# A planned attention, Fourier and channel-mixing kernel: weight signs by VectorE on 16-bit halves, the first masks added by TensorE, a new order

## The chip, the cores and the metric

One core of a Trainium2 chip. The metric is the device time of the program in microseconds (us), the median of the runs. Engines are named as the profile names them: PE is TensorE (PEld its weight loads), DVE is VectorE, ACT is ScalarE, POOL is GpSimd, SP is SyncE, which issues nearly all DMAs.

## The reference

```
scores = q @ k.T / 8                       # 8 batches, 8 heads, 576 tokens, 64 wide
scores = where(mask, scores, -1e9)         # heads 0-3: the last 32 tokens; heads 4-7: every 32nd token, both causal
x      = softmax(scores) @ v               # heads side by side: 8 x 576 x 512
u      = x + real(fft(fft(x, axis=tokens), axis=channels))
un     = (u - mean(u)) / sqrt(var(u) + 1e-6)
out    = u + relu(un @ w1) @ w2            # w1 512 x 2048, w2 2048 x 512, both float64
```

## The kernel before

Heads are taken in pairs: pairs 0 and 1 have the local mask, pairs 2 and 3 the strided one. Of eight batches the first three do attention in float32 (`scores32`, `att_first` for batch 0, `att_pair32` for batches 1 and 2), the others with split 16-bit operands. A pair is a chain: load q, k and v; scores on PE (L556); `weigh` on DVE scales the scores in PSUM and adds the mask (L783), takes the maximum of each window (L790) and subtracts it (L792, on DVE or POOL); exp on ACT; turn on PE; copy on ACT; values on PE; normalise on DVE (L807 to L820); store to the scratch tensor xd in DRAM. Pair 1 of batch 0 is called s_1, o_1, xo_1 below.

When all four pairs of a batch are in xd, the batch is read back as `xa`, and in reversed token order as `xb` by four gathers that POOL issues (L867). `fft_batch` forms E = xa + xb and O = xa - xb (L877), folds them, and PE multiplies by the two transform tables (A, L1020 and L1023 for batch 0; then B). The sums give u; `norm` normalises 128 rows, splits them in two 16-bit parts and turns them by DMA (L1141) into uT. A chunk is 256 rows: 8 `up` steps on PE (L1347, tile ph) and 8 `down` steps (L1387, tile acc). There are 18 chunks; from chunk 15 on, the `Folded` form with other products is used.

The weights arrive as float64 words. `weights(wi, i, m)` turns m pieces of 128 x 512 into float32 bits: ACT scales the high words by a power of two (c1, L1180); a shift of the low words (cl, L1184 on ACT or L1186 on DVE); the sign (sg, L1191 on ACT or a copy on DVE), written as 16 bits into the upper half of each low word; and DVE joins the words (c2, L1197). A pair of pieces (m = 2) has 1024 elements to a partition, a single one 512. PE sums squares of them (gram, L1224), and from these scales ACT and DVE split each weight into two 16-bit parts (L1263, L1266 for w1; L1299, L1302 for w2). All of w1 has to be split before all `up` steps of chunk 0 can run, all of w2 before its `down` steps. While a gram bank is open and the planner sees PE idle, `rest` (L1232) puts in matmuls that add zero.

What sets the order: `Order.run`, at build time, takes steps from threads, each step with an engine, a duration from the source, buffers to get and put, and events; it picks the step that can start first, ties within a window settled by each thread's bias. A step with `alt` can go to a second engine if its duration plus a bias is better. Durations and biases stand in the table `P` and in the `op(...)` calls. Every engine then runs its list in that order, so a step waits for all steps listed ahead of it on its engine. While a step of POOL lasts, the planner keeps most DVE steps back.

```
yield op("V", 1.2 if local else 0.97, get="sm", put="big qk", note=f"weigh {nm}")
o = op("A", 1.15 if m == 2 else 0.69, note=f"sg{z} {wi} {i}", alt=dict(V=(0.62 * m, P["Lsg"])))
o = op("G", 3.45, get="f6", sets=f"O{b}", note=f"O {b}", alt=dict(V=(1.78, P["LO"])))
```

Of the kernel before, what the change touches and what calls it, by code (L numbers as in the profile page):

```python
# [288 lines left out]
def body(ctx: ExitStack, tc: tile.TileContext, a, out):  # L289
# [288 lines left out]
    def att_pair32(b, hp):  # L578
# [34 lines left out]
        yield op("V", 1.05 if local else 0.77, note=f"max {nm}")
        next(g_)
        o = op("V", 1.07 if local else 0.8, note=f"sub {nm}", alt=dict(G=(1.9 if local else 1.38, P["Lsub"])))
        yield o
        g_.send(o)
# [44 lines left out]
    def att_first(sp, pw):  # L662
# [50 lines left out]
        def scores(hp, acc):  # L713
            local = hp < 2
            yield op("T", 0.97 if hp < 2 else 0.84, get="acc" if acc else "big", need=f"q{hp}", sets=f"sc{hp}", note=f"scores {hp}")
# [1133 lines left out]
```

## Time and profile before

| | |
|---|---|
| time, median of 3 runs | 954.75 us (951.97 to 955.89) |
| profiled execution | 950.99 us, span of its instructions 949.1 us |
| PE busy | 913.1 us, 96% of the span |
| DVE, ACT, POOL busy | 694.6 us, 524.6 us, 293.9 us |
| mean granted TensorE clock | 0.981 of full speed |
| moved by DMA | 108.40 MB |

The profiled execution is 1.9 us longer than its span, and 3.76 us shorter than the median of the runs. A busy PE includes the matmuls that add zero. The span falls in a stretch up to the first `up` step of chunk 0, in which weights are converted and batch 0 is brought through attention and transform, and a long stretch in which PE works through the chunks with the other batches' attention in between.

### The profile page before, as it was taken

The numbers are of one execution on the slowest core, as the hardware profiler recorded it, in microseconds if no ns is written. First come the engines' busy times: TensorE is split into PE (matmuls) and PEld (weight loads), VectorE is DVE, ScalarE is ACT, GpSimd is POOL, SyncE is SP. The second block draws the span as 40 slices with busy tenths as digits, with TensorE's granted clock in tenths as the row PEclk, the third lists the DMA queues.
The fourth block names the chain that finished last, engine by engine and source line by source line (L and its number), as shares of the span: only waits on it lengthen the run. The fifth ranks groups of instructions, "written<-read, shape, count | busy, mean of one in ns | idle before, by whom it ended". The sixth has DMA issues, their size and how long they took to land.

```text
span 949.1 us, 25301 instructions
## 1 busy us (share of the span) xinstructions
PE 913.1 (96%) x10583; PEld 673.1 (71%) x10585; DVE 694.6 (73%) x1333; ACT 524.6 (55%) x995; POOL 293.9 (31%) x314
## 2 busy tenths in 40 slices
PE   7688989999999999999999999999999999999997
PEld 6566776666776667666776676667766767699986
DVE  5576777768786786749676866595869889978655
ACT  3878976356573655645646565556433444455542
POOL 0110224124322342334224422452144226525120
PEclk9978899999999999999999999999999999999999
DMA  9878366514344634374336263632250102011100
GB/s 302 269 279 255 126 170 219 179 40 148 95 117 116 156 84 123 98 177 94 97 88 185 73 145 87 186 88 95 55 131 1 45 8 56 17 52 25 41 23 23
DMA packets 140370, 108.40 MB, mean 114 GB/s; under 512 B 108256, under 2 KB 118752, under 8 KB 140256
## 3 DMA queue, kind: packets, MB, share of 16 engines
q1 hardware_dynamic: 137696, 98.40, 37.7%
q0 software_dynamic: 2560, 8.39, 2.6%
q8 instruction: 83, 1.36, 0.6%
q14 instruction: 31, 0.25, 0.1%
HBM read 64.26 MB, written 18.89 MB: 88 GB/s over the span
## 4 chain that ended last, share of the span: by engine, by line
PE 86%; ACT 5%; DVE 4%; issue 2%; DMA 2%; POOL 1%; SPq 0%; DVEq 0%; ACTq 0%; POOLq 0%
PE acc L1387 32%; PE ph L1347 32%; PE acc L1674 5%; PE f L1531 3%; PE B L999 2%; PE A L976 2%; PE s L471 1%; PE o L502 1%; DMA q<-in_qk 1%; PE f_0x L1531 1%; PE f_2x L1531 1%; ACT W L1191 1%; ACT sa L1191 1%; PE o L509 1%; PE s L556 1%
## 5 line engine op out<-in xcount | busy, mean ns | idle before, releaser
L1347 PE MATMUL ph<-uT,W 128*128 128x256 f16 x2880 | 328.7, 273 | 0.7 <-DMA uT<-hb 0.7
L1347 PEld LDWEIGHTS <-W 128*128 128x128 f16 x2880 | 278.9, 98 | 42.7 <-DMA uT<-hb 0.8
L1387 PE MATMUL acc<-W,hb 128*128 128x512 f16 x1344 | 302.4, 379 | 0.0
L1366 POOL TENSOR_TENSOR hb<-hf,hb 128x512 f16<-128x512 f32 x112 | 144.5, 1290 | 330.3 <-ACT hb L1364 233.9
L1387 PEld LDWEIGHTS <-hb 128*128 128x128 f16 x1344 | 128.6, 98 | 142.8
L1363 ACT ACTIVATE hf<-ph 128x512 f32<-128x512 f32 x120 | 71.3, 594 | 143.6 <-PE ph L1347 99.5
L1364 ACT ACTIVATE hb<-ph 128x512 f16<-128x512 f32 x112 | 66.3, 592 | 0.0
L1674 PEld LDWEIGHTS <-tail 128*128 128x128 f16 x504 | 48.3, 98 | 6.5 <-issue 1.3
L1441 DVE TENSOR_TENSOR fold<-fold,W 128x512 f32<-128x512 f32 x64 | 51.9, 834 | 0.2
L433 ACT ACTIVATE kt<-qk,sc 128x576 f16<-128x576 f32 (+1 forms) x40 | 29.4, 788 | 13.5 <-DVE sc L389 12.4
L1531 PEld LDWEIGHTS <-tail 128*128 128x128 f16 x576 | 34.6, 98 | 1.7 <-issue 0.7
L1674 PE MATMUL acc<-fold,tail 128*128 128x256 f16 x288 | 35.5, 273 | 0.0
L448 DVE SCALAR_TENSOR_TENSOR kt<-qk,sc,kt 128x576 f16<-128x576 f32 (+1 forms) x40 | 33.2, 869 | 3.2 <-ACT kt L433 3.1
L1100 ACT ACTIVATE pq<-B,fcm 128x128 f32<-128x128 f32 (+7 forms) x105 | 27.2, 382 | 15.1 <-PE B L999 14.2
L1644 DVE TENSOR_TENSOR tail<-hb,tail 128x512 f16<-128x512 f32 (+1 forms) x46 | 31.8, 720 | 3.3 <-ACT tail L1641 3.1
L1232 PE MATMUL gram<-oneb,zero 128*128 128x128 bf16 x386 | 31.9, 251 | 1.2 <-issue 1.1
L989 DVE SCALAR_TENSOR_TENSOR AT<-A,AT 128x290 f16<-128x290 f32 (+3 forms) x35 | 15.2, 481 | 23.5 <-ACT AT L984 20.8
L1618 POOL TENSOR_TENSOR hb<-hb 128x256 f32<-128x256 f32 x20 | 15.8, 796 | 52.7 <-ACT hb L1604 17.2
L1232 PEld LDWEIGHTS <-zero 128*128 128x128 bf16 x386 | 29.5, 116 | 3.3 <-issue 2.5
L1121 POOL TENSOR_TENSOR rstd<-mv,negh 128x1 f32<-128x1 f32 x30 | 20.1, 676 | 34.7 <-DVE mv L1118 30.1
L792 DVE TENSOR_TENSOR sm<-sm,mx 128x594 f32<-128x594 f32 (+1 forms) x32 | 30.2, 942 | 0.4
L1139 DVE TENSOR_TENSOR unp<-un,unp 128x512 f16<-128x512 f32 x28 | 23.1, 825 | 10.0 <-ACT unp L1136 9.9
(306 smaller groups left out, 1516.9 us busy)
## 6 DMA issues: line engine op xcount, KB each, us to landing
qk<-in_qk SPq DMA_DIRECT2D x28, 592.0 KB
out<-ub SPq DMA_DIRECT2D x32, 256.0 KB
sa<-in_w SPq DMA_DIRECT2D x14, 512.0 KB
vn<-in_vl SPq DMA_DIRECT2D x10, 432.0 KB
W<-in_w SPq DMA_DIRECT2D x8, 512.0 KB
xd<-xo SPq DMA_DIRECT2D x16, 256.0 KB
xa<-xd SPq DMA_DIRECT2D x8, 512.0 KB
vn<-in_vs SPq DMA_DIRECT2D x10, 384.0 KB
```

What stands on the lines that cost most here:

```text
L448: V.scalar_tensor_tensor(out=lo, in0=src, scalar=f, in1=hi, op0=ALU.mult, op1=ALU.subtract)
L792: on(o).tensor_tensor(out=sm, in0=sm, in1=mx[:, 0:nb].rearrange("p (g o) -> p g o", o=1).to_broadcast([128, nb, w]), op=ALU.subtract)
L1232: T.matmul(idle[-1][:, 0:128], zerb, oneb, start=False, stop=False)
L1347: T.matmul(ph[:, i, :], W1[:, 4 * (f0 // 512) + d, x, f0 % 512 : f0 % 512 + 128], self.uhl[y][:, d, :], start=(n == 0), stop=(n == 11))
L1363: A.activation(hf, ph, AF.Relu, scale=HS)
L1364: A.activation(hh, ph, AF.Relu, scale=HS)
L1366: G.tensor_tensor(out=hl, in0=hf, in1=hh, op=ALU.subtract)
L1387: T.matmul(self.acc[s], (hh, hl)[x][:, i, 128 * s : 128 * s + 128], W2[:, f, 1 - y, :], start=(f == 0 and n == 0), stop=(f == 15 and n == 2))
L1441: on(e).tensor_tensor(out=w, in0=w if x is None else x, in1=y, op=ALU.add if f else ALU.subtract)
L1531: T.matmul(dst[:, 128 * f : 128 * f + 128], w(x, i)[:, 128 * f : 128 * f + 128], u(y, i), start=opens and f == 0 and n == 0, stop=closes a ...
L1644: on(o).tensor_tensor(out=lo, in0=src, in1=hi, op=ALU.subtract)
L1674: T.matmul(dst, hop[:, x, j, 128 * i : 128 * i + 128], w(y, i), start=bank not in opened, stop=q == 3 and z in (6, 5, 3, 4) and i == 1 and ...
```

## The change

1. `weights`: the sign is no longer a float copy on DVE but, on 16-bit halves, an AND of the highest half of each word with 0x8000, written to the same place. On ACT it stays as it was. The planner's durations for sg become 2.5 (pair) and 1.35 (single) on ACT, 0.7 and 0.46 on DVE.
2. `scores32`: ahead of the scores of a pair PE writes the mask into the PSUM bank by bf16 matmuls of the identity with the mask's upper halves (3 for a local pair, 2 for a strided one), and the scores are added to it. A new function `peak` takes the maximum out of PSUM and subtracts it while leaving PSUM; the factor 0.125 moves into ACT's exp. `weigh` is left to batches 3 to 7. q and k are given back after the scores and not after `weigh`; the PSUM tile is held until the subtraction. The steps of batch 0 now need the identity and the masks to be loaded ahead of the scores.
3. `P` has new numbers throughout: no pairs in w2 (`M1=()`), other staging buffers for w2's pieces (`S1`), the bias LO of O on DVE from -8.618 to 23.142, and others. With it the order of all engines is new.

```
-    WV=0.068, WA=0.22, WG=1.14, WT=0.212, SL=0.0, SLD=1.819, np=3, AL=3.136, SG=2.918, Lcl=0.163, Lsg=2.308, Lfs=-0.071,
-    Lwl=6.215, Lul=-7.046, LO=-8.618, LE=4.916, Lc2=-2.015, LSD=-15.747, Lsub=4.379, Lsub0=20.296, Lrt=11.607, Lu=4.507,
+    WV=0.068, WA=0.04, WG=0.925, WT=0.185, SL=0.0, SLD=0.818, np=3, AL=3.136, SG=2.918, Lcl=-0.177, Lsg=0.763,
+    Lfs=-1.314, Lwl=-2.525, Lul=-9.275, LO=23.142, LE=5.158, Lc2=-1.062, LSD=-13.902, Lsub=20.832, Lsub0=28.983,
...
+        eye = half16(ident)
+        if local:
+            m = half16(mloc.rearrange("p g w -> p (g w)"))
+            masks = [(0, m), (512, m[:, w:]), (512 + 4 * w, m[:, w : 2 * w])]
+        else:
+            m = half16(mstr)[:, 0:GR].rearrange("p (o w) -> p o w", o=1).to_broadcast([128, NG2, w])
+            masks = [(0, m), (512, m)]
+        for o, m in masks:
+            T.matmul(ps[:, o : o + (m.shape[1] if local else per * w)], eye, m, start=o % 512 == 0, stop=False, skip_group_check=True)
...
-                    T.matmul(ps[rows(local, g, h), off[g] : off[g] + w], qk[hs, st : st + 64], qk[hs, S + st : S + st + w], start=True, stop=True)
+                    T.matmul(ps[rows(local, g, h), off[g] : off[g] + w], qk[hs, st : st + 64], qk[hs, S + st : S + st + w], start=False, stop=True, skip_group_check=True)
...
-        yield op("V", 1.2 if local else 0.97, get="sm", put="big qk", note=f"weigh {nm}")
+        yield op("V", 1.1 if local else 0.8, note=f"peak {nm}")
+        g_ = peak(nm, ps, n, wk, lambda: apool.tile([128, NQB * WIN], F32, tag="sm", name=f"sm{nm}", bufs=1))
+        next(g_)
+        yield op("V", 1.15 if local else 0.9, get="sm", put="big", note=f"less {nm}")
...
+    def peak(nm, ps, nb, w, sm):
+        per = (nb + 1) // 2
+        mx = small.tile([128, 2 * NG2], F32, tag="mx", name=f"mx{nm}")
+        pv = ps.rearrange("p (x c) -> p x c", x=2)[:, :, 0 : per * w].rearrange("p x (g w) -> p x g w", w=w)
+        V.tensor_reduce(out=mx[:, 0 : 2 * per].rearrange("p (x g) -> p x g", x=2), in_=pv, axis=AX.X, op=ALU.max)
+        yield sm
+        sm = (sm() if callable(sm) else sm)[:, 0 : nb * w].rearrange("p (g w) -> p g w", w=w)
+        for x, g0, g1 in ((0, 0, per), (1, per, nb)):
+            top = mx[:, g0:g1].rearrange("p (g o) -> p g o", o=1).to_broadcast([128, g1 - g0, w])
+            V.tensor_tensor(out=sm[:, g0:g1], in0=pv[:, x, 0 : g1 - g0], in1=top, op=ALU.subtract)
+        yield sm
...
-        o = op("A", 1.15 if m == 2 else 0.69, note=f"sg{z} {wi} {i}", alt=dict(V=(0.62 * m, P["Lsg"])))
+        o = op("A", 2.5 if m == 2 else 1.35, note=f"sg{z} {wi} {i}", alt=dict(V=(0.7 if m == 2 else 0.46, P["Lsg"])))
...
-            V.tensor_copy(sg, wh.bitcast(F32))
+            ws = stg.bitcast(U16).rearrange("p (n t) -> p n t", t=4)
+            V.tensor_scalar(ws[:, :, 1], ws[:, :, 3], 0x8000, None, op0=ALU.bitwise_and)
```

ACT, from the conversion of the first weights on: W_89 is the staging tile of w1, q_111 and q_113 the next two, L1191 (L1208 in the new numbering) the sign. Before:

```order
L1180 ACTIVATE W_89<-W_89 128x1024
L745 COPY pt_1_123<-pT_1_453 96x1024
L1191 ACTIVATE W_89<-W_89 128x1024
L745 COPY pt_1_123<-pU_1_495 96x128
L1191 ACTIVATE W_89<-W_89 128x1024
L1180 ACTIVATE W_89<-W_89 128x1024
L1184 ACTIVATE W_89<-W_89 128x1024
L1263 ACTIVATE W_89<-W_90,scl 128x2x512 x2
L1191 ACTIVATE W_89<-W_89 128x1024
L1180 ACTIVATE W_89<-W_89 128x1024
L1184 ACTIVATE W_89<-W_89 128x1024
L1191 ACTIVATE W_89<-W_89 128x1024
```

and now:

```order
L750 COPY pt_1_123<-pT_1_416 96x1024
L1198 ACTIVATE W_89<-W_89 128x1024
L750 COPY pt_1_123<-pU_1_463 96x128
L1208 ACTIVATE W_89<-W_89 128x1024
L1198 ACTIVATE W_89<-W_89 128x1024 x2
L1202 ACTIVATE W_89<-W_89 128x1024
L1198 ACTIVATE q_111<-q_111 128x1024
L1202 ACTIVATE q_111<-q_111 128x1024
L1281 ACTIVATE W_89<-W_90,scl 128x2x512 x2
L1198 ACTIVATE q_113<-q_113 128x1024
L1281 ACTIVATE W_89<-W_90,scl 128x2x512 x4
```

Of the signs ACT keeps one pair here. In the whole program ACT had all 23 of them (9 pairs, 14 single) and now has 1 pair and 6 single; DVE has 5 pairs and 14 single.

SP's DMA queue, behind the loads of batch 0: xd_95 is the scratch tensor of batch 0, xo_3, xo_2, xo_0 and xo_1 the finished pairs. Before:

```order
L1168 DMA W_89<-in_w 128x512 x5
L829 DMA xd_95<-xo_3_133 18x11x64 x2
L829 DMA xd_95<-xo_3_133 18x10x64
L829 DMA xd_95<-xo_3_133 18x11x64 x2
L829 DMA xd_95<-xo_3_133 18x10x64
L829 DMA xd_95<-xo_2_132 18x11x64 x2
L829 DMA xd_95<-xo_2_132 18x10x64
L829 DMA xd_95<-xo_2_132 18x11x64 x2
L829 DMA xd_95<-xo_2_132 18x10x64
L1168 DMA W_89<-in_w 128x512
L815 DMA xd_95<-xo_0_130 128x4x128
L817 DMA xd_95<-xo_0_130 64x64 x2
```

and now:

```order
L1186 DMA W_89<-in_w 128x512 x8
L1186 DMA q_111<-in_w 128x512 x2
L847 DMA xd_95<-xo_3_133 18x11x64 x2
L847 DMA xd_95<-xo_3_133 18x10x64
L847 DMA xd_95<-xo_3_133 18x11x64 x2
L847 DMA xd_95<-xo_3_133 18x10x64
L1186 DMA q_113<-in_w 128x512 x2
L847 DMA xd_95<-xo_2_132 18x11x64 x2
L847 DMA xd_95<-xo_2_132 18x10x64
L847 DMA xd_95<-xo_2_132 18x11x64 x2
L847 DMA xd_95<-xo_2_132 18x10x64
L833 DMA xd_95<-xo_0_130 128x4x128
```

All 12 weight loads now stand ahead of the stores of pairs 2, 0 and 1; ten of them stand ahead of the first store, where five did.

DVE at the transform of batch 0 (E, O, tmp and FD are its tiles, L1197 the joining of weight words, L1266 the second half of a split weight). Before:

```order
L1197 SCALAR_TENSOR_TENSOR W_90<-q_111 128x1024
L1266 SCALAR_TENSOR_TENSOR W_89<-W_90,scl,W_89 128x2x512
L877 TENSOR_TENSOR E_752<-xa_591,xb_593 128x1536
L877 TENSOR_TENSOR O_755<-xa_591,xb_593 128x1536
L877 TENSOR_TENSOR tmp_757<-E_752 128x3x255
L1266 SCALAR_TENSOR_TENSOR W_89<-W_90,scl,W_89 128x2x512
L877 TENSOR_TENSOR tmp_757<-tmp_757 128x3x128
L1197 SCALAR_TENSOR_TENSOR W_90<-q_113 128x1024
L877 TENSOR_TENSOR FD_758<-tmp_757 128x3x64 x2
L877 TENSOR_TENSOR E_752<-O_755 128x3x255
L877 TENSOR_TENSOR FD_758<-E_752 128x3x127 x2
L877 TENSOR_TENSOR FD_758<-tmp_757 128x3x128
```

and now:

```order
L1284 SCALAR_TENSOR_TENSOR W_89<-W_90,scl,W_89 128x2x512 x3
L895 TENSOR_TENSOR E_758<-xa_676,xb_678 128x1536
L895 TENSOR_TENSOR tmp_762<-E_758 128x3x255
L895 TENSOR_TENSOR tmp_762<-tmp_762 128x3x128
L895 TENSOR_TENSOR FD_763<-tmp_762 128x3x64 x2
L895 TENSOR_TENSOR E_758<-O_760 128x3x255
L895 TENSOR_TENSOR FD_763<-E_758 128x3x127 x2
L895 TENSOR_TENSOR FD_763<-tmp_762 128x3x128
L1204 TENSOR_SCALAR sa_12_794<-sa_12_794 128x512
L1211 TENSOR_SCALAR sa_12_794<-sa_12_794 128x512
L1215 SCALAR_TENSOR_TENSOR W_90<-sa_12_794 128x512
```

O has left DVE: in all eight batches it stands on POOL, next behind the gathers. No weight step stands between E and the last FD, where one L1266 and one L1197 stood.

On PE the counts are: 30 mask matmuls more, 378 matmuls of L1232 where 386 were, everything else the same in number. Ahead of the first `up` step the scores of pairs 3 and 2 of batch 1 stand as before; those of pair 0 have moved behind it.

## Rows read from the trace of the kernel before

**Rows 1.** The page, part 5 (costliest groups): the matmuls that add zero
```profile
L1232 PE MATMUL gram<-oneb,zero 128*128 128x128 bf16 x386 | 31.9, 251 | 1.2 <-issue 1.1
```

**Rows 2.** Busy time by stretch; columns: stretch, length, engines, PEclk, DMA share, GB/s
```profile
0.00:98.94 98.94, 75.91 (x1031) 61.87 (x1033) 65.25 (x128) 70.04 (x79) 10.50 (x16) 0.84 0.85 277
98.94:180.00 81.06, 76.14 (x906) 56.13 (x905) 59.94 (x114) 55.64 (x80) 22.58 (x20) 0.99 0.53 160
180.00:820.00 640.00, 640.00 (x7095) 445.47 (x7094) 479.87 (x918) 338.01 (x691) 224.60 (x240) 1.00 0.39 100
820.00:949.10 129.10, 121.09 (x1556) 109.61 (x1553) 89.51 (x177) 60.92 (x148) 36.20 (x39) 0.99 0.11 32
```

**Rows 3.** Line L1191, the sign on ACT: ns min/median/max; who waited, us and times
```profile
L1191 ACT ACTIVATE sa<-sa x14: 1329/1348/1409, 65.8 to 114.9; 128x512 f16<-128x512 f32 x14
...
L1191 ACT ACTIVATE W<-W x4: 2472/2490/2501, 26.1 to 41.6; 128x1024 f16<-128x1024 f32 x4
...
  DVE W L1197: 19.9, 17
```

**Rows 4.** DVE groups by line and form, first 180 us: busy us, mean ns
```profile
L792 DVE TENSOR_TENSOR sm<-sm,mx 128x864 f32<-128x864 f32 x6 | 7.3, 1215 | 0.1
L790 DVE TENSOR_REDUCE mx<-sm 128x9 f32<-128x864 f32 x6 | 6.3, 1051 | 0.1
...
L1197 DVE SCALAR_TENSOR_TENSOR W<-W 128x1024 int32<-128x1024 int32 x4 | 4.9, 1226 | 6.5 <-ACT W L1191 6.5
...
L783 DVE SCALAR_TENSOR_TENSOR sm<-s,mloc 128x480 f32<-128x480 f32 x6 | 3.9, 654 | 2.9 <-PE s L556 2.8
...
L1186 DVE TENSOR_SCALAR sa<-sa 128x512 int32<-128x512 int32 x8 | 3.5, 460 | 0.0
L783 DVE SCALAR_TENSOR_TENSOR sm<-s,mloc 128x384 f32<-128x384 f32 x6 | 3.3, 549 | 0.0
...
L1186 DVE TENSOR_SCALAR W<-W 128x1024 int32<-128x1024 int32 x2 | 1.4, 700 | 1.8 <-DMA W<-in_w 1.8
```

**Rows 5.** Timeline of SP's DMA queue and of POOL: start, length, what
```profile
10.08 7.53 SPq L1168 DMA_DIRECT2D W<-in_w  x5
19.00 8.64 SPq L829 DMA_DIRECT2D xd<-xo  x12
...
33.91 1.18 SPq L817 DMA_DIRECT2D xd<-xo  x2
...
39.11 1.14 POOL L867 DMA_INDIRECT xa<-xd,ridx  x1 [36.32 <-DMA q<-in_w]
```

**Rows 6.** From E of batch 0 to the first `up` step: timelines, one stretch
```profile
50.91 1.75 DVE L877 TENSOR_TENSOR E<-xa,xb 128x1536 f32<-128x1536 f32 x1
...
62.46 0.70 PE L1020 MATMUL A<-f32a,FD 33*65 33x290 f32 x2
...
62.40:74.10 11.70, 11.65 (x34) 6.27 (x32) 6.35 (x11) 10.81 (x14) 1.15 (x2) 0.55 0.65 221
...
89.45 0.55 DVE L1129 TENSOR_SCALAR un<-ub,mv,rstd 128x512 f32<-128x512 f32 x1
...
92.34 0.60 ACT L1136 CAST hb<-un 128x512 f16<-128x512 f32 x1
...
98.94 3.82 PE L1347 MATMUL ph<-uT,W 128*128 128x256 f16 x24
```

**Rows 7.** POOL's and DVE's elementwise steps at the same time: line L1366, and timelines
```profile
L1366 POOL TENSOR_TENSOR hb<-hf,hb x112: 1144/1160/3062, 143.5 to 820.2; 128x512 f16<-128x512 f32 x112
...
159.62 1.17 POOL L1366 TENSOR_TENSOR hb<-hf,hb 128x512 f16<-128x512 f32 x1
...
159.69 2.03 DVE L792 TENSOR_TENSOR sm<-sm,mx 128x864 f32<-128x864 f32 x1
```

**Rows 8.** Chain that ended last: twelve matmuls of 512 columns; scores of a local pair
```profile
130.74 1.07 PE s L556 x36
...
164.25 2.59 PE acc L1387 x12
```

More of the change, by code (lines that the diff above doesn't have):

```diff
@@ L15 @@
 U32 = mybir.dt.uint32
+U16 = mybir.dt.uint16
 AF = mybir.ActivationFunctionType
@@ L159 @@
 AL, SG = P["AL"], P["SG"]
-PORT = ("st", "weigh", "max", "out", "AL", "y1", "y2", "norm", "vlo", "fin", "SD", "u0", "u1", "u2", "rstd", "pad", "ones", "zero", "xb", "c5", "scales")
+PORT = ("st", "peak", "less", "weigh", "max", "out", "AL", "y1", "y2", "norm", "vlo", "fin", "SD", "u0", "u1", "u2", "rstd", "pad", "ones", "zero", "xb", "c5", "scales")
 class Op:
@@ L605, in att_pair32 @@
         spawn(values())
-        yield op("T", 0.97 if local else 0.84, get="big", at=end, note=f"scores {nm}", slack=SL)
+        yield op("T", 1.4 if local else 1.16, get="big", put="qk", at=end, note=f"scores {nm}", slack=SL)
         ps = psbig(f"s{nm}")
         wk, off = scores32(ps, qk, local, n)
-        yield op("V", 1.2 if local else 0.97, get="sm", put="big qk", note=f"weigh {nm}")
-        sm = apool.tile([128, NQB * WIN], F32, tag="sm", name=f"sm{nm}", bufs=1)
-        g_ = weigh(nm, ps, local, n, wk, off, 0.125, sm)
+        yield op("V", 1.1 if local else 0.8, note=f"peak {nm}")
+        g_ = peak(nm, ps, n, wk, lambda: apool.tile([128, NQB * WIN], F32, tag="sm", name=f"sm{nm}", bufs=1))
+        next(g_)
+        yield op("V", 1.15 if local else 0.9, get="sm", put="big", note=f"less {nm}")
         sm = next(g_)
[L613 to L617, printed above, removed]
         yield op("A", 0.92 if local else 0.7, get="" if local else "pbt", put="" if local else "sm", note=f"exp {nm}")
         if local:
-            A.activation(sm, sm, AF.Exp)
+            A.activation(sm, sm, AF.Exp, scale=0.125)
             pb, nt = sm, NQB
         else:
-            A.activation(pbd[:, 0:NG, 0:GR], sm, AF.Exp)
+            A.activation(pbd[:, 0:NG, 0:GR], sm, AF.Exp, scale=0.125)
             pb, nt = pbd.rearrange("p (g e) c -> p g (e c)", e=2), NG2
@@ L714, in scores @@
             local = hp < 2
-            yield op("T", 0.97 if hp < 2 else 0.84, get="acc" if acc else "big", need=f"q{hp}", sets=f"sc{hp}", note=f"scores {hp}")
+            yield op("T", 1.4 if hp < 2 else 1.16, get="acc" if acc else "big", need=f"q{hp} id " + ("mloc" if local else "mstr"), sets=f"sc{hp}", note=f"scores {hp}")
             ps = wide(acc, f"s0_{hp}")
@@ L718, in scores @@
             w, off = scores32(ps, q0s[hp], local, nb)
-            yield op("V", 1.2 if local else 0.97, put="acc" if acc else "big", need="mloc" if local else "mstr", note=f"weigh {hp}")
-            g = weigh(f"0_{hp}", ps, local, nb, w, off, 0.125, sms[hp])
+            yield op("V", 1.1 if local else 0.8, note=f"peak {hp}")
+            g = peak(f"0_{hp}", ps, nb, w, sms[hp])
+            next(g)
+            yield op("V", 1.15 if local else 0.9, put="acc" if acc else "big", note=f"less {hp}")
             sm = next(g)
-            yield op("V", 1.05 if local else 0.77, note=f"max {hp}")
-            next(g)
-            o = op("V", 1.07 if local else 0.79, note=f"sub {hp}", alt=dict(G=(1.95 if local else 1.4, P["Lsub0"])))
-            yield o
-            g.send(o)
             yield op("A", 0.93 if local else 0.72, sets=f"e{hp}", note=f"exp {hp}")
             if local:
-                A.activation(sm, sm, AF.Exp)
+                A.activation(sm, sm, AF.Exp, scale=0.125)
                 pbs[hp] = sm
             else:
-                A.activation(pbs[hp][:, 0:NG, 0:GR], sm, AF.Exp)
+                A.activation(pbs[hp][:, 0:NG, 0:GR], sm, AF.Exp, scale=0.125)
                 pbs[hp] = pbs[hp].rearrange("p (g e) c -> p g (e c)", e=2)
@@ L788, in weigh @@
         yield sm
-        mx = small.tile([128, NG], F32, tag="mx", name=f"mx{nm}")
+        mx = small.tile([128, 2 * NG2], F32, tag="mx", name=f"mx{nm}")
         V.tensor_reduce(out=mx[:, 0:nb], in_=sm, axis=AX.X, op=ALU.max)
```

22 lines of the change are left out of this document (11 added, 11 removed).

## The prediction

> **What bounds the kernel now.** I read the busy times by stretch first [rows 2]. From 180 to 820 us PE is busy in every one of the 640 us, so there the time is the sum of PE's work, and a faster DVE or ACT gives nothing. PE stands idle only ahead of that: 98.94 - 75.91 = 23.0 us up to the first `up` step of chunk 0, 81.06 - 76.14 = 4.9 us from there to 180, and 129.1 - 121.1 = 8.0 us after 820, most of it behind the last matmul. To the 23.0 come 31.9 us of matmuls that add zero [rows 1], nearly all in the first stretch, and the clock granted there, 0.84 of full speed. So whatever this change can win is won by letting the first `up` step start ahead of its 98.94 us; what it can lose anywhere is PE work added, or a PE wait made, after that.
>
> In the first stretch no engine is full: ACT is busy for 70.0 of 98.9 us, DVE for 65.3, and DMA for 0.85 of the time [rows 2]. The order of a chain across them decides, and ACT's longest steps are in it: a sign takes ACT 2.49 us for a pair and 1.35 for a single piece, and DVE's joining of the words waited 19.9 us in 17 waits for it [rows 3].
>
> **The change, part by part.**
>
> *Signs.* ACT loses 9 pairs and 14 singles and keeps 1 and 6: 8 x 2.49 + 8 x 1.35 = 30.7 us less. On DVE 5 pairs and 14 singles are new. No row shows that operation (an AND, two bytes written in every eight). The nearest is L1186, DVE's shift of one operand with a constant on the same tile and step: 0.70 and 0.46 us; the upper end for DVE is L1197, which takes one element at a time, 1.23 us, and far beyond it ACT's own 2.49 [rows 3, 4]. I take L1186: 5 x 0.70 + 14 x 0.46 = 9.9 us more for DVE.
>
> *Masks.* Twelve matmuls of 512 columns take 2.59 us, 0.216 each [rows 8]. A local pair adds 480 + 384 + 96 = 960 columns, 0.41 us; a strided one 2 x 324 = 648, 0.27 us. Ahead of the first `up` step these stand in PE's idle time. After it are the scores of pairs 0 and 1 of batch 1 and of four pairs of batch 2: 4 x 0.41 + 2 x 0.27 = **2.2 us** of PE work in the full stretch. That the scores now wait for masks to load costs nothing in batch 0: pair 0's mask is issued between q of pairs 0 and 1, and PE has pair 1's q to wait for anyway.
>
> *DVE in attention.* A local pair costs 0.654 + 0.549 + 1.051 + 1.215 = 3.5 us [rows 4]. Now it is a maximum out of PSUM over 960 elements, which no row shows: between 1.05 us (864 elements, SBUF) and 1.2 us (that, scaled by 960/864), I take 1.16; and two subtractions out of PSUM at the L783 prices, 1.20. That is 1.1 us less for each of six local pairs, and an estimated 0.7 for each of six strided ones (594 elements). All in all 11 us, which pays for DVE's signs. Off the path, both count nothing by themselves.
>
> *Path to E.* In the new queue ten weight loads are ahead of the first store of batch 0 and twelve ahead of the last. Loads went out at 7.53/5 = 1.51 us, stores at 8.64/12 = 0.72, the last small ones at 0.59 [rows 5]. From 10.08: ten loads to 25.1, six stores to 29.5, two loads to 32.5, six stores to 36.8, six small ones to 40.3. Before, the last store was out at 33.91 + 1.18 = 35.1 and the gathers began 4.0 us later, at 39.11 [rows 5]. If loads past the fifth find room sooner, the last store is out at about 35 again. So the gathers come 0 to 5.2 us later, less up to 2 because no load is left just ahead of the last stores. I take E 1 us later than 50.91 (range -2 to +5). DVE's own queue ahead of E now holds five signs, one L1197 and three L1266 more, 8.6 us, less 3.6 for four shorter pairs; I count the 5 us as worked off while DVE would have waited for ACT's signs, and the range covers it otherwise.
>
> *E to A.* From E to A before: 62.46 - 50.91 = 11.55 us [rows 6]. L1197 and L1266 no longer stand in it (1.23 + about 1.28), and O's 1.75 us leave DVE: 7.3. But O now runs on POOL next to E. The trace shows what that does: a subtraction on DVE that began 0.07 us after a step of POOL took 2.03 us, the other five of its form (7.3 - 2.03) / 5 = 1.05; it waited out POOL's step [rows 4, 7]. O on POOL lasts, from 1.16 us for 512 elements [rows 7], up to 3 x 1.16 = 3.5 us, and not under DVE's 1.75; I take 3.2, and half of it, 1.5 us, as DVE's wait. E to A: 8.8 us. The Trainium skill, "SBUF — State Buffer", section "Who interferes with whom", says the same and speaks against this move: a DVE instruction with two SBUF inputs and a GpSimd instruction that reads SBUF hold the same port for the whole instruction, and the one that issues second "fully blocks". By it all of O's 3.2 us could fall on DVE and A come 1.7 us later than I have it; without it A would come 1.5 us sooner. The row agrees, by one case of 0.98 us. A starts at 50.91 + 1 + 8.8 = 60.7, **1.8 us sooner**.
>
> *A.* From 62.4 to 74.1 the granted clock is 0.55 of full speed, that is 1.2 GHz for nearly all of it, with PE busy throughout [rows 6]; before it PE had stood idle in short gaps between added zeros. At 2.4 GHz the 11.65 us would be 0.55 x 11.65 = 6.4. The new list has 146 matmuls of zero directly ahead of A where 8 behind 27 stood, so the clock may be up; or a gap still follows. 0 to 5.2 us, I take half, **2.6 us**.
>
> *A to the first `up` step.* 98.94 - 74.1 = 24.8 us. In it, `un` of the second half was done at 89.45 + 0.55 = 90.0, and ACT came to its cast at 92.34, from signs and scalings queued ahead [rows 6]: 2.3 us. Sums of u and the scaling of AT stood behind the same steps. Between 1 us (DVE's new work takes half back) and 7, I take **4 us**.
>
> *After the first `up` step.* ACT was busy 55.6 of 81 us [rows 2], most of it in the first third; with four signs fewer here I give PE 1.5 of its 4.9 us idle. Against that stand the masks, 2.2 us, and the scores of pair 0 of batch 1, moved behind the first `up` step: 1.07 us [rows 8].
>
> Sum: -1.8 - 2.6 - 4.0 = -8.4, so the first `up` step at 90.5; -8.4 - 1.5 + 2.2 + 1.0 = -6.7. The profiled execution of 950.99 would take 944.3. It lies 3.76 below the median of 954.75, so for the median of the runs: **948 us**.
>
> What is late next: the split of w2 ahead of `down`. It has the conversion of 12 pieces behind the first `up` step in both lists, and PE has 12 `up` steps and batch 1's attention to do until then, where it had 10.
>
> **The rivals.**
>
> *A, the front is held by transfers.* The stores go out 5.2 us later, A keeps its slow clock. Then E to A as above gives A 2.4 us later than before, -4 behind it, the first `up` step at 97.3: -1.6 - 1.5 + 3.2 = 0.1, the median at 955. For it: DMA is at 0.85 in the first stretch. Against it: the same weights have to come either way, and the loads sent early are the ones the split needs. Chance 0.22.
>
> *B, all of it comes.* Gathers 2 us sooner (A 4.8 sooner), full clock 5.2, 7 us behind A: -17, with 3 us less idle and 3.2 more work -16.8 at most, 938; of the usual size 942. Chance 0.12.
>
> *C, slower: the sign costs DVE what it costs ACT,* because what makes ACT's 2.49 us out of the 1.2 of a plain pass is the narrow write, which stays. Five pairs ahead of E cost 5 x 1.79 = 9.0 us, two singles on the way to the `up` step 1.8: -8.4 + 10.8 = +2.4. Nine more behind it are 8 us on a DVE that is busy for 59.9 of 81 us [rows 2], of which I let 3 reach PE: 2.4 + 3 - 1.5 + 3.2 = +7, 962. It decides from about 1.9 us a pair on. Against it: the slowest of DVE's own forms at this size is at 1.23 us [rows 4]. Chance 0.07.
>
> *D, a bank held longer.* The scores' PSUM tile was free after `weigh`, 1.2 us, and is now held through maximum and subtraction, 2.36. There are two such banks, and PE's next step of attention needs one. If PE waits the 1.16 us for each of the eight pairs of batches 1 and 2, 9.3 us go: +2.6, 957. Against it: `up` and `down` steps lie between, and PE had no wait of this kind in the full stretch. Chance 0.10, a part of it with further stalls and over 959.5.
>
> **How the numbers follow.** My forecast has 0.49, with its own range 944 to 952 from the ends of E, clock and O. A measurement of this kernel can tell about 0.5%, 4.8 us, from no change: faster is under 950.0, slower over 959.5. Faster: 0.45 of the forecast and all of B, 0.57. Same: 0.04 of the forecast, A's 0.22 and 0.06 of D, 0.32. Slower: C and 0.04 of D, 0.11. For the range I reach to B's usual size and beyond A and D's plain case: 940 to 957.
>
> **What would show it.** Right: the first `up` step at 88 to 93 us, A at 60 to 62 with a granted clock over 0.7, the sign on DVE at 0.7 and 0.46 us, ACT busy some 31 us less, DVE some 14 us less (O's eight go to POOL), no PE idle from 180 to 820. Wrong: the first `up` step at 96 or later (A); a sign over 1.9 us (C); waits of PE for DVE's subtraction (D); or PE idle inside the full stretch, which none of my terms has.

## The result and the profile after

The changed kernel takes 964.44 us (median of 4 runs, 963.98 to 965.10); the kernel before took 953.36 us beside it (4 runs, 951.75 to 955.89). The ratio is 1.0114, with a 95% interval of 1.0087 to 1.0142: the change makes it **slower by 1.1%**, 11 us. Forecast were 948 us, within 940 to 957. The profiled execution of 964.66 us has a span of 962.6 us, 13.5 us more than the span before, and a mean granted clock of 0.975.

The page of after, part 1, busy time by engine:

```profile
PE 923.9 (96%) x10605; PEld 675.2 (70%) x10607; DVE 720.2 (75%) x1333; ACT 494.9 (51%) x983; POOL 342.2 (36%) x326
```

ACT is busy 29.7 us less, as forecast (31). DVE is busy 25.6 us more, where 14 less were forecast. PE is busy 10.8 us more and idle 38.7 us instead of 36.0.

Where the time lies is read from the busy time by stretch of after (columns as in [rows 2]):

```profile
0.00:95.31 95.31, 75.34 (x997) 59.90 (x1000) 69.56 (x130) 45.95 (x61) 16.27 (x17) 0.82 0.77 258
95.31:180.00 84.69, 78.96 (x945) 57.30 (x943) 63.05 (x110) 50.42 (x82) 25.54 (x19) 0.98 0.57 180
180.00:260.00 80.00, 80.00 (x892) 55.59 (x890) 61.98 (x126) 42.35 (x93) 35.28 (x39) 1.00 0.42 117
260.00:280.00 20.00, 17.31 (x190) 12.65 (x190) 12.58 (x35) 13.10 (x35) 4.97 (x8) 0.91 0.36 88
280.00:420.00 140.00, 140.00 (x1688) 96.81 (x1687) 101.68 (x195) 76.04 (x148) 48.54 (x46) 1.00 0.45 111
420.00:440.00 20.00, 17.27 (x157) 9.92 (x155) 6.52 (x10) 6.17 (x12) 8.52 (x9) 0.91 0.67 191
440.00:820.00 380.00, 380.00 (x4095) 263.58 (x4094) 298.42 (x538) 192.99 (x395) 158.29 (x143) 1.00 0.34 89
```

The first `up` step starts at 95.31 us instead of 98.94 [rows 6]: 3.6 us are won. Then PE, which before had no idle time from 180 to 820 us [rows 2], stands idle for 2.7 us in each of two stretches of 20 us, and in both the granted clock falls to 0.91. In all other stretches after 180 PE is full, as before. PE's waits of after from 180 to 830 us name the two (what PE waited for: us, times, longest):

```profile
PE A L994 <- DVE AT L1007: 2.7, 1, 2.7
PE s L472 <- issue: 2.2, 5, 0.5
PE acc L1405 <- issue: 0.5, 1, 0.5
```

The second and third are one place, a block of scores on 16-bit operands. The timeline of PE and POOL of after there (start, length, what, idle time ahead and what ended it):

```profile
421.23 0.54 PE L472 MATMUL s<-kt 64*64 64x54 f16 x44
421.95 0.25 PE L472 MATMUL s<-kt 64*64 64x54 f16 x5 [0.19 <-issue]
422.71 0.25 PE L472 MATMUL s<-kt 64*64 64x54 f16 x6 [0.51 <-issue]
...
425.67 4.45 PE L1405 MATMUL acc<-W,hb 128*128 128x512 f16 x12 [0.51 <-issue]
...
421.37 1.00 POOL L885 DMA_INDIRECT xa<-xd,ridx  x1 [0.15 <-issue]
```

The block of 66 small matmuls runs at its usual speed for 0.54 us. From then on PE starts 4 to 6 of them every 0.75 us, idle in between though no semaphore holds it ("issue"). POOL's first gather began 0.14 us after the block. The block takes 3.75 us from the start of its first matmul to the start of its last, the measure for such blocks from here on, against 0.56 elsewhere; the granted clock falls behind it, and twelve `down` matmuls take 4.45 us where 2.6 to 2.75 are usual. The same happens at 151.87 us, outside that window, to the float32 scores of a pair of batch 2: 36 matmuls take 3.9 us (0.8 elsewhere), beside the gathers of batch 1, and the 12 behind them 4.45.

So the 13.5 us are: -3.6 at the first `up` step, about +3 for the masks and the moved scores behind it, +4.6 at 152 us, +4 at 262 us (AT, below), +6 at 421 us. That makes 14, within the reading of such places.

### The profile page after: what moved, and what is told of

It is laid out like the page before. It is cut to its first block, busy times and chain, and to the rows that moved or that the text cites. A ratio compares the mean times of both kernels' runs of the same rounds, so it can differ in the third digit from the quotient of the medians.

```text
span 962.6 us, 25341 instructions
## 1 busy us (share of the span) xinstructions
PE 923.9 (96%) x10605; PEld 675.2 (70%) x10607; DVE 720.2 (75%) x1333; ACT 494.9 (51%) x983; POOL 342.2 (36%) x326
## 5 line engine op out<-in xcount | busy, mean ns | idle before, releaser
L1384 POOL TENSOR_TENSOR hb<-hf,hb 128x512 f16<-128x512 f32 x112 | 157.2, 1404 | 311.3 <-ACT hb L1382 227.8
L1459 DVE TENSOR_TENSOR fold<-fold,W 128x512 f32<-128x512 f32 x64 | 55.9, 901 | 0.1
L1636 POOL TENSOR_TENSOR hb<-hb 128x256 f32<-128x256 f32 x26 | 22.9, 894 | 53.9 <-DVE hb L1636 31.4
L1139 POOL TENSOR_TENSOR rstd<-mv,negh 128x1 f32<-128x1 f32 x30 | 22.2, 744 | 52.3 <-DVE mv L1136 52.3
L449 DVE SCALAR_TENSOR_TENSOR kt<-qk,sc,kt 128x576 f16<-128x576 f32 (+1 forms) x40 | 36.9, 964 | 4.3 <-ACT kt L434 4.2
L1662 DVE TENSOR_TENSOR tail<-hb,tail 128x512 f16<-128x512 f32 (+1 forms) x48 | 34.9, 757 | 3.9 <-ACT tail L1659 3.5
L1110 DVE TENSOR_TENSOR rt<-pq 128x257 f32<-128x257 f32 (+1 forms) x42 | 16.1, 423 | 26.6 <-ACT pq L1118 17.5
L895 POOL TENSOR_TENSOR O<-xa,xb 128x1536 f32<-128x1536 f32 x8 | 29.1, 3637 | 18.7 <-PE acc L1405 16.0
L484 ACT ACTIVATE sm<-sm 128x594 f32<-128x594 f32 (+1 forms) x20 | 16.2, 810 | 31.7 <-DVE sm L810 31.7
L1250 PE MATMUL gram<-oneb,zero 128*128 128x128 bf16 x378 | 29.3, 243 | 2.7 <-issue 2.7
```

Source lines behind the costliest of these rows:

```text
L449: V.scalar_tensor_tensor(out=lo, in0=src, scalar=f, in1=hi, op0=ALU.mult, op1=ALU.subtract)
L1250: T.matmul(idle[-1][:, 0:128], zerb, oneb, start=False, stop=False)
L1384: G.tensor_tensor(out=hl, in0=hf, in1=hh, op=ALU.subtract)
L1459: on(e).tensor_tensor(out=w, in0=w if x is None else x, in1=y, op=ALU.add if f else ALU.subtract)
L1662: on(o).tensor_tensor(out=lo, in0=src, in1=hi, op=ALU.subtract)
```

## The experiments

In each kernel below the order of all engines is written out as a list, the one the planner made for after (names in a_) or before (b_), so that only the edit moves anything. Ratios are to the kernel before, run beside it. In the expectations, G is the theory that POOL's gathers, issued beside a block of small matmuls, starve PE; its rivals are that other transfers, the added masks or the signs cost the time.

**a_hold: the gathers kept off the scores.** Where POOL would issue the gathers of batches 1 and 4, it waits for the last score matmul of the block.

```
             gather xb / xa of batch b, part n
+            hold(b, n)      # b in (1, 4), n == 0: the gather depends on the scores' last matmul
```

> The changed kernel in its own order, but POOL's four gathers of batches 1 and 4 wait for the last matmul of the scores that they overlapped (pair 0 of batch 2 at 151.9 us, pair 2 of batch 5 at 421.2 us). Theory G (PE's run of small score matmuls starves while POOL issues gathers): both blocks of scores come back to about 0.8 and 0.6 us from 3.9 and 3.8, the PE waits put down to issue there go, no drop of the granted clock behind them, and the time falls by 4.5 + 6 = 10 us to about 954. Rival P (the place in PE's program, whatever POOL does): the blocks stay at 3.9 and 3.8 us, 964.

954.22 us, ratio 1.003 [1.0014, 1.0046]. PE's timeline of a_hold:

```profile
149.82 1.04 PE L568 MATMUL s<-qk 64*64 64x96 f32 x36
...
255.97 0.38 PE L994 MATMUL A<-csin,FH 128*127 128x145 f16 x3 [2.70 <-DVE AT L1007]
...
414.64 0.75 PE L472 MATMUL s<-kt 64*64 64x54 f16 x66
```

Both blocks run through without a gap. The ratio falls from 1.0114 to 1.003, 8 us by the ratios and 10 by the medians (7 and 8 against the unchanged order run again, a_again below): two waits, each ahead of one batch's gathers, take away most of the slowdown. The wait for AT is untouched.

**b_hold: the same coincidence made in the kernel before.** The gathers of batches 2, 3 and 5 are held until they fall beside score blocks.

```
+            hold(b, n)      # b in (2, 3, 5), n == 0: depends on a matmul just ahead of the scores
```

> The kernel before in its own order, but the gathers of batches 2, 3 and 5 wait for the matmul ahead of the step of PE that stands ahead of scores (blocks at 221.5, 320.2 and 514.5 us, 0.56 us each before), so that POOL issues gathers while PE does these scores. Theory G: these three blocks take 3 to 4 us, with waits put down to issue, 4 to 6 us each: 953 + 12 to 18 = 965 to 971. Rival P: they stay at 0.56 us; the later gathers may delay E of batches 3 and 5 by some 2 us each, 953 to 957.

952.42 us, 1.0005 [0.9987, 1.0022]. POOL's and PE's timelines of b_hold at the third block:

```profile
515.86 0.94 POOL L867 DMA_INDIRECT xb<-xd,ridx  x1 [0.30 <-issue]
...
515.55 1.31 PE L471 MATMUL s<-kt 64*64 64x54 f16 x66
```

A miss. The blocks took 0.66, 0.67 and 1.12 us instead of 0.56: a trace of the effect and no more. The kernel before, too, has a block of scores among its gathers, and it is not slowed (36 matmuls, starts 0.80 us apart from first to last). Its PE and POOL there:

```profile
155.44 1.04 PE L556 MATMUL s<-qk 64*64 64x96 f32 x36
...
155.12 0.95 POOL L867 DMA_INDIRECT xb<-xd,ridx  x1 [0.30 <-DMA vlx<-in_v]
156.38 1.98 POOL L867 DMA_INDIRECT xb<-xd,ridx  x1 [0.30 <-issue]
```

Standing beside a gather is needed in after (a_hold), but it is not enough.

**a_o_dve: O back on DVE,** in all eight batches, nothing else moved.

```
-  O b: engine POOL
+  O b: engine DVE
```

> The changed kernel in its own order, O of all eight batches back on DVE at the places where POOL had them. Theory O (O on POOL holds up DVE's steps of two SBUF inputs): E takes 1.75 us in place of 5.00, the main part of A starts 1 to 3 us sooner than 63.0, the wait of 2.7 us of PE for AT at 262.8 goes with the clock drop behind it: 958 to 960. Rival: DVE has 14 us more of work, A starts no sooner and the wait for AT stays, since ACT's steps ahead of it set it: 964 or more. The two slow blocks of scores stay in either.

949.75 us, 0.9982 [0.9964, 1.0]: against after's 1.0114 some 13 us less by the ratios and 15 by the medians, more than expected. DVE's and PE's timelines of a_o_dve:

```profile
51.59 1.76 DVE L895 TENSOR_TENSOR E<-xa,xb 128x1536 f32<-128x1536 f32 x1 [0.98 <-DMA xb<-xd,ridx]
...
61.66 1.61 PE L1041 MATMUL A<-f32a,E 128*65 128x145 f32 x4 [3.35 <-POOL E L895]
...
254.98 0.38 PE L994 MATMUL A<-csin,FH 128*127 128x145 f16 x3 [1.43 <-DVE AT L1007]
411.98 1.02 PE L472 MATMUL s<-kt 64*64 64x54 f16 x66
```

E takes 1.76 us (5.00 in after), the main part of A starts 1.4 us sooner than in after, the wait for AT is halved, and no slower clock follows it. The block at 412 us takes 0.83 us, though a gather started 0.14 us into it, as in after. So with O on DVE the blocking in the front is gone, and in this profile the starved blocks are gone too. That moving O is what frees them is not shown: in a_fill below, which has the same move, the block at 151.54 us is starved in the profiled execution (2.69 us instead of 0.80), though its gathers stand as far from it as those of a_o_dve stand from its block at 150.10 us, which is not slowed. The time between the starts of block and gather does not say which block is starved.

**a_hold_o: both edits.**

```
+            hold(b, n)
-  O b: engine POOL
+  O b: engine DVE
```

> Both edits together, the gathers held and O on DVE. Theory G and theory O right: 10 + 4 to 6 us less than the changed kernel, 948 to 950, below the kernel before. Only G: 954. Only O: 959. Neither: 964.

949.87 us, 0.9982 [0.9966, 0.9998], the same as a_o_dve alone: with O on DVE there is nothing left for the hold to win.

**a_again: the list of after, unchanged,** as a control.

```
   (no edit)
```

> The changed kernel as it is, with its order written out as a list; a control. If the two slow blocks of scores (3.9 and 3.8 us) belong to this order they are there again and the time is 964 as before, in most runs; if they come and go from run to run, the runs scatter between 953 and 965.

961.89 us, 1.0104 [1.0062, 1.0146], with runs from 957.99 to 965.55. PE's timeline of the profiled execution (957.99 us), second block and the `down` step behind the first:

```profile
418.13 0.26 PE L472 MATMUL s<-kt 64*64 64x54 f16 x6 [0.47 <-issue]
...
154.54 2.76 PE L1405 MATMUL acc<-W,h 128*128 128x512 f16 x12
```

Both blocks are starved again (3.78 and 3.62 us), so they belong to this order. The slower clock behind them is not always there (12 matmuls in 2.76 us here); that may be part of the several us between single runs.

**a_dma: other transfers kept off the second block.** The loads of q, k and v of batch 5 and of xa, which SP issues at 420 to 421.5 us, wait for the scores' last matmul.

```
+        late5(dma_start(qk, ...)), late5(dma_start(vn, ...))   # batch 5, pair 0
+        late5(dma_start(xa, ...))                              # batch 4
```

> The changed kernel in its own order, gathers where they were, but the three loads that SP issues at 420.4, 421.0 and 421.5 us (qk and vn of pair 0 of batch 5, xa of batch 4) wait for the last matmul of the scores of pair 2 of batch 5. Theory G2 (gathers slow the scores only when other transfers run beside them): the block at 421 takes 0.6 to 0.9 us in place of 3.6 to 3.8, the one at 151 stays at 3.8; some 4 us less than the changed kernel. Theory G1 (the gathers alone do it there): the block at 421 stays at 3.6 to 3.8.

963.28 us (2 runs), 1.0108 [1.0078, 1.0139]. PE and SP in a_dma:

```profile
420.46 0.26 PE L472 MATMUL s<-kt 64*64 64x54 f16 x6 [0.48 <-issue]
...
424.99 0.35 SPq L403 DMA_DIRECT2D qk<-in_qk  x1
```

The block is starved again (2.96 us) while these loads start only at 424.99. It is 0.7 to 0.8 us shorter than in after and a_again, and the block of batch 2 still takes 3.73 us. These three loads of SP are not what starves it; other transfers were not held.

**b_masks: the masks alone,** in the order of before.

```
+  masks by TensorE ahead of the scores; peak and less in place of weigh
```

> The kernel before in its own order with the masks alone: they are laid into PSUM by matmuls, and maximum and subtraction read PSUM (the subtraction directly behind the maximum). Theory: only the masks behind the first up step count, 2.2 us: 951.9 + 2.2 = 954. Rival: DVE's 11 us less in attention bring E and the first up step 2 to 4 us sooner, 951 or less. Rival D of the prediction: PE waits for a bank of scores, up to 9 us more, 961.

959.67 us, 1.0069 [1.0047, 1.0092], 7 us slower, and the first `up` step comes at 104.3 us. PE's waits of b_masks:

```profile
PE s L561 <- DVE sm L789: 2.6, 2, 2.1
PE s L561 <- DMA ident<-in_ident: 1.9, 1, 1.9
```

In this order the identity is loaded behind the second q, and the first scores wait for it: a wait that I had counted as nothing. The other row is rival D: PE waits for a bank until the subtraction is out of PSUM. After's order has placed both so that they cost little.

**b_signs: the signs alone.** 7 pairs and 11 single pieces take their sign on DVE, in the order of before.

```
-  sg: engine ACT
+  sg: engine DVE     # 7 pairs, 11 single
```

> The kernel before in its own order with the signs alone: 7 pairs and 11 single pieces of 9 and 14 have their sign from DVE by an AND, at the places where ACT had them. ACT loses 7 x 2.49 + 11 x 1.35 = 32 us, DVE has 7 x 1.33 + 11 x 0.74 = 17 us more. Theory (ACT's signs hold the front up): the first up step 3 to 4 us sooner than 98.9, time 948 to 949. Rival (at 1.33 us a pair DVE takes back what ACT gives): first up step within 1 us, 951 to 953.

952.57 us, 0.9996 [0.9972, 1.002]. PE and DVE in b_signs:

```profile
118.12 1.51 PE L632 MATMUL t<-ident,pbt 128*128 128x128 f32 x6 [3.02 <-DVE sm L783]
...
112.90 0.73 DVE L1193 TENSOR_SCALAR sa<-sa 128x512 uint16<-128x512 uint16 x1
116.86 1.11 DVE L783 SCALAR_TENSOR_TENSOR sm<-s,mloc 128x480 f32<-128x480 f32 x2
```

The first `up` step comes at 96.5 us, 2.4 us sooner, and then PE waits 3.02 us for attention's step on DVE, which came to it late, behind the signs. Moved without a new order, the signs gain nothing.

**a_sg_act: all signs back on ACT,** in the good version a_hold_o.

```
-  sg: engine DVE
+  sg: engine ACT
```

> The changed kernel in its own order with gathers held and O on DVE (949.9 us), and all signs back on ACT: 5 pairs and 14 single pieces more there, 5 x 2.49 + 14 x 1.35 = 31 us, and 17 us less on DVE. Theory (the signs on DVE are what brings the front forward): the first up step 4 us later or more, 954 or more. Rival (the front is held by transfers, E and the clock): within 1 us, 950.

962.08 us, 1.0091 [1.0066, 1.0116]. The first `up` step of a_sg_act on PE:

```profile
101.99 2.35 PE L1365 MATMUL ph<-uT,W 128*128 128x256 f16 x16 [1.94 <-DMA uT<-hb]
```

Against a_hold_o's 0.9982 the signs on DVE are worth 1.1% in the new order, 10.4 us by the ratios and 12.2 by the medians, and the first `up` step comes 8.0 us later without them (94.0 in a_hold_o). As in b_signs the order was not planned anew, and here E, too, starts 5.4 us later (57.22 instead of 51.78): this is the price of undoing the move in an order planned with it, not its gain over an order planned without it, which no run has.

**a_fill: more zeros around A's first matmul,** in a_o_dve, against A's slow clock.

```
-  zeros ahead of A: 146
+  zeros ahead of A: 196, and rest(50) behind its FD matmul
```

> The changed kernel in its own order with O on DVE (as the run before) and 100 more matmuls of zero: 50 ahead of A's first matmul and 50 behind it, where PE stands idle for 3.3 and 3.4 us. Theory (the idle gaps are what lowers the clock for A and B): no drop of the granted clock from 57 to 80 us, A's matmuls in half the time, 62 to 74 becomes 62 to 68, the first up step 3 to 5 us sooner, 945 to 947. Rival (the clock falls with zeros too, or DVE and POOL set the end of B anyway): 949 to 951.

948.32 us, 0.9953 [0.9929, 0.9976]. Windows of a_fill ahead of and in A:

```profile
56.00:62.00 6.00, 4.96 (x77) 4.20 (x74) 5.15 (x9) 0.59 (x3) 1.78 (x3) 1.00 0.99 349
62.00:74.00 12.00, 11.08 (x36) 6.67 (x37) 6.49 (x14) 3.96 (x9) 1.33 (x2) 0.59 0.69 253
```

The granted clock is 1.00 while the zeros run and falls in A again: PE still stood idle for 1.18 us at 62.7, waiting for POOL's side sums in E. The faster median is not the profiled execution's: that took 952.94 us, the slowest of ten, and in it the block of batch 2 is starved:

```profile
153.00 0.41 PE L568 MATMUL s<-qk 64*64 64x96 f32 x4 [0.32 <-issue]
```

**a_best: no gap ahead of A.** As a_hold_o, with the side sums of batch 0 on DVE (those for A's next matmul first), and 54 zeros more ahead of A's first matmul and 36 behind it.

```
-  SD0 0, SD257 0: engine POOL
+  SD0 0, SD257 0: engine DVE, SD0 first
-  zeros ahead of A: 146
+  zeros ahead of A: 200, and rest(36) behind its FD matmul
```

> The changed kernel with gathers of batches 1 and 4 held, O on DVE, the two side sums of batch 0 on DVE with those that A needs first ahead, and 54 + 36 more matmuls of zero ahead of A and behind its first matmul. Theory (each edit's part adds up): A's main part 1 us sooner than 61.7, at the full clock for at least its first half, 2 to 4 us off 949.9: 945 to 948, faster than the kernel before by 0.5 to 0.8%. Rival (clock drops all the same, A's sooner end is lost behind it): 949 to 950.

943.10 us, **0.990 [0.9878, 0.9921]: it beats both kernels**. A window of a_best over A, and PE's timeline:

```profile
60.00:74.00 14.00, 13.88 (x95) 9.86 (x92) 11.73 (x29) 9.46 (x16) 0.00 (x0) 1.00 0.87 321
...
85.41 2.79 PE L1365 MATMUL ph<-uT,W 128*128 128x256 f16 x24 [0.76 <-DMA uT<-hb]
```

The granted clock is 1.00 in all of A, which ends at 66.4 us, and the first `up` step comes at 85.41, 9.9 us ahead of after and 13.5 ahead of before. What the side sums and what the zeros give of this was not tried apart.

**b_best: the same front in the kernel before.** Its side sums on DVE, 51 zeros more.

```
-  zeros ahead of two steps of gram: 73 and 27
+  zeros ahead of two steps of gram: 104 and 47
-  SD0 0, SD257 0: engine POOL
+  SD0 0, SD257 0: engine DVE
```

> The kernel before in its own order with the front edits of the best run alone: the two side sums of batch 0 on DVE, those that A needs first ahead, and 51 more matmuls of zero in PE's two idle gaps of 1.9 and 1.3 us ahead of A. Theory (these edits give what they give with either kernel): A at the full clock for most of it, the first up step 5 us sooner or more, 944 to 947. Rival (they pay only in the changed kernel's order, since here DVE's joins and ACT's signs still stand between A and the first up step): 949 to 953.

952.56 us, 1.0017 [1.0, 1.0034]. PE's timeline of b_best:

```profile
70.67 0.76 PE L1023 MATMUL A<-f32a,O 128*128 128x145 f32 x4
...
100.38 1.86 PE L556 MATMUL s<-qk 64*64 64x96 f32 x36 [3.34 <-DMA qk<-in_qk]
```

A ran at full clock (its steps take 0.70 to 0.76 us, where in the profile of before most take 1.23 to 1.33). That can't be put down to the edit: b_hold, which changes nothing ahead of A, has it too, and so have b_masks and b_signs (granted clock 0.89 and 0.95 from 62 to 74 us, 0.56 before). The window over A of b_hold:

```profile
62.00:74.00 12.00, 10.34 (x73) 6.81 (x72) 6.92 (x16) 9.86 (x13) 2.83 (x4) 0.93 0.67 248
```

Yet the first `up` step came at 100.86 us in b_hold, 1.9 later than before. In b_best it came at 102.2: behind A, PE waited for the joining of words (L1197, up to 2.20 us) and 3.34 us for a load of q and k. In this order a faster A meets weights and loads that are not ready. That the signs on ACT are the reason is likely for the weights, but no run shows it by itself.

## Why the prediction was wrong, point by point

**The step that failed** is the base of the sum: that behind the first `up` step the time is PE's work, and that an edit that adds none costs nothing there. The sum put waits of PE in that stretch at nothing ("PE idle inside the full stretch, which none of my terms has"). Behind the first `up` step it had -1.5 + 2.2 + 1.0 = +1.7 us; the profiled span has 13.5 + 3.6 = +17.1. Of this, a_hold shows 7 to 10 us to come from two blocks of scores that met POOL's gathers, one at 421 us and one at 152, ahead of the full stretch; in its profile the time from the first `up` step on is 5.7 us longer than before. What such a meeting costs could not be read from before: the only such block found in its trace ran at its usual speed (155.44 us, under b_hold).

The second part in that stretch comes with O on POOL, whose cost the sum looked for ahead of A alone. POOL and DVE of after at 230 us, and PE at the wait for AT:

```profile
230.34 3.45 POOL L895 TENSOR_TENSOR O<-xa,xb 128x1536 f32<-128x1536 f32 x1
230.57 3.85 DVE L488 SCALAR_TENSOR_TENSOR pbt<-sm,pbt 128x594 f16<-128x594 f32 x1 [1.65 <-ACT pbt L486]
...
262.79 0.59 PE L994 MATMUL A<-csin,FH 128*127 128x145 f16 x3 [2.69 <-DVE AT L1007]
```

A step of DVE that takes 0.78 us in the mean in a_o_dve took 3.85 beside O. At 262 us PE waited 2.69 us for AT, which DVE and ACT make. With O on DVE (a_o_dve) this wait is 1.43 us; in a_hold, which leaves O on POOL, it stays at 2.70. So half of it comes with O; the way from one to the other, over many steps, was not traced.

**DVE's time,** forecast 14 us down, went 25.6 up. DVE groups of after (busy us, mean ns, idle before and releaser):

```profile
L488 DVE SCALAR_TENSOR_TENSOR pbt<-sm,pbt 128x594 f16<-128x594 f32 x10 | 14.1, 1407 | 12.0 <-ACT pbt L486 12.0
...
L389 DVE TENSOR_SCALAR ib<-ib 128x3 int32<-128x3 int32 x20 | 12.3, 615 | 0.7
```

Before, these two were 7.7 and 4.9 us with the same counts; in a_o_dve they are 7.8 and 4.2, so the stretching goes with O on POOL. It lies in single steps. Of the 20 of L389, three elements to a partition, the median is unchanged at 0.17 us, and the longest took 3.12, at 630.49 us beside O. In seven of O's eight runs on POOL one step of DVE lasted 2.9 to 3.3 us longer than alone, E of batch 0 among them: some 22 us, for about 15 that had left DVE. In a_o_dve, with O back, DVE is busy 704.6 us, 15.7 less than in after; of the other 10 us that after has over before, the sign's price makes 9 (below). So nothing of the forecast's "O's eight go to POOL" lightened DVE.

**E to A** was forecast at 8.8 us, counted to A's first matmuls (L1020 of before, L1038 of after). They came 58.30 - 51.08 = 7.22 us behind E. But A's main part, on E and O, then stood: it began 11.96 us behind E, where before it had begun 63.09 - 50.91 = 12.18 behind. DVE, POOL and PE of after there, and the main part's first row of before (L1023):

```profile
51.08 5.00 DVE L895 TENSOR_TENSOR E<-xa,xb 128x1536 f32<-128x1536 f32 x1
...
50.49 3.98 POOL L895 TENSOR_TENSOR O<-xa,xb 128x1536 f32<-128x1536 f32 x1 [2.71 <-DMA xb<-xd,ridx]
...
58.30 1.20 PE L1038 MATMUL A<-f32a,FD 33*65 33x290 f32 x2 [3.20 <-ACT FD L922]
63.04 1.19 PE L1041 MATMUL A<-f32a,E 128*65 128x145 f32 x3 [3.54 <-POOL E L895]
...
63.09 1.26 PE L1023 MATMUL A<-f32a,E 128*65 128x145 f32 x4
```

So the forecast followed the wrong end of the path. The main part waits for the side sums that POOL adds into E, which came as late as before (from 62.26 us on, 62.14 before) and for which the sum has no term. Even in a_o_dve PE waits 3.35 us for them, and the main part begins 10.07 us behind E.

E itself came 0.2 us later than before, where I had 1. But it took 5.00 us instead of 1.75: 3.25 us of blocking where I took 1.5, half of O. O had issued 0.59 us ahead; E ended 1.6 us after O, a little under its own 1.75. The rule of the Trainium skill, "SBUF — State Buffer", section "Who interferes with whom" (the later of the two "fully blocks"), is what this row shows; by it I had 1.7 us more, which is nearly what came (1.75 more). My halving was the wrong choice between two bounds.

**A's clock** was forecast to give 2.6 us and gave none. The window over A of after:

```profile
63.00:75.00 12.00, 11.96 (x36) 6.97 (x37) 6.43 (x13) 3.98 (x9) 0.67 (x1) 0.50 0.40 139
```

That is 1.2 GHz throughout. The 146 zeros stood ahead of A in the list, but PE was idle for 3.20 and 3.54 us between them and A (above). In a_fill the low level came behind a gap of 1.18 us, and in a_best, with no gap, A ran at 2.4 GHz. A gap alone doesn't decide: in b_best A ran at 2.4 GHz behind one of 1.70 us (61.69 us of before has one of 1.27, and A at 1.2 GHz behind it). What decides is not shown. The term also read the low clock of before as a property of its order, from one profile; b_hold has the same front and the high clock, and its first `up` step came no sooner.

**The sign on DVE** (line L1211 of after: ns min/median/max):

```profile
L1211 DVE TENSOR_SCALAR sa<-sa x13: 730/750/1727, 67.9 to 128.8; 128x512 uint16<-128x512 uint16 x13
L1211 DVE TENSOR_SCALAR W<-W x3: 1323/1326/1328, 21.8 to 33.9; 128x1024 uint16<-128x1024 uint16 x3
```

1.33 and 0.75 us, where I took 0.70 and 0.46 from L1186, the nearest by form. It goes a little over the price of L1197 (1.23), my upper end for DVE [rows 4]. For 5 pairs and 14 single pieces that is 5 x 0.63 + 14 x 0.29 = 7.2 us. The planner had been given the same 0.7 and 0.46. Rival C (ACT's 2.49, deciding from 1.9) is refuted, and a_sg_act shows the move to be worth 10 to 12 us in this order even so, against undoing it.

**Right** were ACT's 30 us and A to the first `up` step: A ended at 74.15 us (74.04 before), so this took 21.2 us instead of 24.9, 3.7 less where 4 were forecast. The first `up` step came 4.8 us later than forecast, and A's end, 74.15 us instead of 69.8 by the sum, is 4.35 of that: E's blocking, the wait for POOL's side sums and A's clock. DVE's steps of a local pair came as forecast, 1.15 us for the maximum and 1.20 for the subtractions (1.16 and 1.20), and the masks a little dearer, 0.52 and 0.39 us a pair (0.41 and 0.27). That the masks wait for loads at no cost holds for this order and not for that of before (b_masks).

**The rivals.** A had the first `up` step at 97.3 us, nearer to 95.31 than my 90.5, and its slow clock for A came true, but it had transfers hold the front: E started only 0.2 us later than before, 0.6 us behind the end of O's wait for a gather. D, a bank held longer, shows in b_masks and not as an added wait in after. B's full clock in the order of after came only in a_best, and so did a front as early as B's.

**What stays open:** what, beside a gather, decides how far a block of small matmuls is slowed. Beside gathers, the blocks of 66 took from 0.66 us to 3.75 and those of 36 from 0.80 to 3.9. The same distance between the two starts gave 3.75 us in after and 0.83 in a_o_dve at the one block, 2.69 in a_fill and 0.80 in a_o_dve at the other. The pattern (a handful of matmuls every 0.75 us, PE waiting for nothing that the profile shows) suggests that PE lacked instructions; no run here tested that. A late load of code is not seen at 421 us: the trace of after has no packet of the instruction queue from 418 to 430 us, and PE runs in full again from 425.67. O on POOL is not needed for the starving (a_fill).

## What to carry to other kernels

A stretch in which one engine is full is no proof that edits elsewhere are free there: look at what each reordering puts beside that engine's densest instructions, and keep another engine's indirect transfers off its runs of small matmuls. Moving a large two-input step from VectorE to GpSimd can move its time only on paper while VectorE works on (VectorE was busy 720.2 us with O on GpSimd and 704.6 with O on VectorE); as an estimate from E and the seven steps above, count the whole step as VectorE's wait. Zeros that are to keep the clock up have to be judged by the granted clock of the work behind them (0.59 in a_fill, 1.00 in a_best), not by their number, and a faster front pays only when what stands behind it is ready.

## What the runs showed of the hardware that was not expected

- Blocks of 36 or 66 small matmuls, 0.8 and 0.56 us alone, took up to 3.9 and 3.75 us beside GpSimd's indirect DMAs, with idle gaps of 0.34 to 0.51 us that no semaphore explains, and with the granted clock sometimes lower behind them. It does not come with every meeting: the block among the gathers of the kernel before (155.44 us) took its usual 0.80 us. What decides is open.
- An AND on 16-bit halves, stepped by eight bytes, takes VectorE 1.33 us for 1024 elements, against 0.70 for a shift of 32-bit words at the same step.
- While O, 128x1536 with two inputs, ran on GpSimd, one VectorE step waited it out, even one on 3 elements to a partition (L389): 3.12 us instead of 0.17. Over its 20 runs the mean of L389 is 0.62 us, 0.25 in the kernel before.
